# Scores of the second batch from q and k in float32: no squares, no scale and no half-precision words of q and k for batch 1, and a new order of all instructions

## The chip, the core and the metric

The kernel runs on one core of one Trainium2 chip. The core has five instruction streams that run beside each other: TensorE (PE in the profile; its weight loads are PEld), VectorE (DVE), ScalarE (ACT), GpSimd (POOL) and SyncE (SP, which here only issues DMAs). Each takes its instructions strictly in the order in which the program holds them, and waits for the others through semaphores. The metric is the device time of one execution in microseconds (us); the figure given for a kernel is the median of several executions.

## The reference

Causal attention with a decay over 8 batches of 8 heads (576 positions, 64 wide), and behind it a two-layer block over all 4608 tokens:

```python
scores = scale * np.matmul(q, k.transpose(0, 1, 3, 2))
cum = np.cumsum(np.log(np.clip(f, 0.0001, 1.0)), axis=-1)
decay = cum[:, :, :, None] - cum[:, :, None, :]
scores = np.where(causal, -1000000000.0, scores + decay)
scores = scores - np.max(scores, axis=-1, keepdims=True)
attn = np.exp(scores)
attn = attn / (np.sum(attn, axis=-1, keepdims=True) + 1e-09)
x = np.matmul(attn, v)            # then (4608, 512), heads beside each other

h = x @ w_in                      # 512 -> 1024
e = np.exp(h - h.max(-1)); sm = e / (e.sum(-1) + 1e-09)
solu = h * sm
ln = (solu - mean(solu)) / sqrt(var(solu) + 1e-06) * g_ln
out = ln @ w_out                  # 1024 -> 512
```

All inputs and the output are float32.

## The kernel before, in words

**Tiling.** Two heads make a pair; there are 4 pairs in a batch and 32 in all (pair p belongs to batch p // 4 and uses the buffers numbered p % 4). The 576 rows of a pair's scores are cut into five tiles of 64, 128, 128, 128 and 128 rows; tile i has 64 + 128 i columns, and the last one's 576 columns are cut into two of 288. That is 64 + 192 + 320 + 448 + 288 + 288 = 1600 columns per head. The two heads of a pair stand on the two halves of the PE's rows, so that their products run side by side. The block behind the attention works on 36 "layers" of 128 tokens: 24 products into the pair of banks `hps` (lines 919 to 921), a chain on DVE, ACT and POOL, a transpose, and 24 products out (lines 989 to 991).

**Number formats.** Products are made of half-precision words: a float32 number is scaled by a power of two and split into a high and a low float16 word, and a product is three passes (high by high, low by high, high by low). For q and k of a batch this takes: the load into one of four buffers `raws` (`load`, line 761), squares that are summed per partition to find the largest size (`squares`, line 673, on ACT at line 681), one scale for the batch (`scale`, line 628, a chain of small DVE instructions at lines 645 to 670 with two small PE products between), and per pair two high words (POOL, through `copied`, line 503) and two low words (DVE, line 774), made by `split_qk` and written to one of four buffers `qk16`. v is treated in the same way (lines 783 and 784).

**Batch 0 is an exception already.** Its q and k are loaded straight into the `qk16` buffers, used there as float32 (`native`, line 757), and its score products are a single float32 pass (line 819). Since the k words of the other batches carry a factor 16 (`QK`), the score step's own factor (line 841) and the rows of `pick` for the decay term (line 435) differ between batch 0 and the rest. The decay term is one more pass with bfloat16 words (line 817, `pick` and `crow`).

**After the scores.** The reduction with mask and smallest value is on DVE (line 840), the exponential on ACT (line 845), sums on POOL (line 851), the reciprocal on DVE (line 852), the high word of the probabilities on ACT or POOL (lines 501, 503), the low word on DVE (line 867). A DMA from the SP queue transposes them (line 510, `t_p`), the PE multiplies with v (line 889), and ACT and DVE make the two words of x (lines 898, 899).

**Order.** Every step is put into a list as an `Op` with an engine, an estimated cost in ns and the steps it depends on. `Plan.schedule` then lays the list out in time with those costs: of the steps that are ready on an engine it takes the one with the lowest number in the table `RANK` (one number for each step, in the order in which the steps are created). Where the plan leaves the PE without work in its first 300 us, it fills the gap with dummy products of the identity (line 1113, 256 columns each), one for each 256 x 0.4525 ns of planned gap (`FILLED`, `COLUMN`). The program that runs is the plan's order; the chip does not follow the plan's times.

**Buffers.** There are four `raws` and four `qk16` buffers. With `raws`, the load of a later batch may run while the scores of the earlier one still read `qk16`. With the float32 form the load itself goes to `qk16`, and it has to wait until the last score product of the pair that used the buffer is done. All loads and transposes are issued by SP in one order.

Of the kernel before, what the change touches and what calls it, by code (L numbers as in the profile page):

```python
# [15 lines left out]
ALU = mybir.AluOpType  # L16
# [27 lines left out]
NRAW, NQK, NS = 4, 4, 6  # L44
# [5 lines left out]
TURN = (1100.0, 22.0, 1700.0, 6.0)  # L50
# [23 lines left out]
class Plan:  # L74
# [308 lines left out]
def tile_kernel(ctx: ExitStack, tc: tile.TileContext, qk, v, f, w_in, w_out, g_ln, out):  # L383
# [48 lines left out]
    def picks():  # L432
        for n in range(2):
            nc.gpsimd.memset(pick[:, n], -8.0 * QK)
        nc.gpsimd.memset(pick[:, 0, :NPAIR], -8.0)
        for h in range(2):
            for n in range(2):
                x = pick[D * h:D * h + D, n]
# [604 lines left out]
    def whole(p, at, due):  # L1043
        if p >= NPAIR:
            split_qk(p, at + due["split"] + AT_P[p][0])
# [112 lines left out]
```

## Time and profile before

| | us |
|---|---|
| median of 3 runs (lowest, highest) | 698.45 (696.26, 700.66) |
| the profiled execution, whole time | 699.97 |
| its span, first to last instruction | 698.2 |
| PE busy (with the dummy products) | 652.0 |
| DVE busy | 573.9 |
| ACT busy | 532.3 |
| POOL busy | 386.7 |

The span is 1.8 us shorter than the whole time of that execution, and that execution is 1.5 us above the median. Busy time is the time in which at least one instruction of the engine was running. A row of a stage table gives a stretch of the span, its length, and for each engine the busy time and in brackets the number of instructions; a row of a group gives line, engine, operation, tiles and shapes, the count behind x, then the busy time of all of them and the mean ns of one, and last the idle time of the engine just ahead of them with what ended it. A row of the timeline gives the start, the length, and a run of like instructions with its count.

### The profile page before, as it was taken

To read this page: it belongs to the slowest core of one execution; us is meant where nothing else is said; L and a number is where in the kernel's file an instruction comes from. 1 tells how busy PE (TensorE), PEld (TensorE's weight loads), DVE (VectorE), ACT (ScalarE), POOL (GpSimd) and SP (SyncE) were. 2 spreads that over 40 slices of the span, in tenths; PEclk is the share of its full clock that TensorE was granted. 3 is DMA by queue.
4 is the path that set the end of the run, shared out by engine and by line. 5 is a ranking of instruction groups with operands and counts; after the bars stand their busy time and mean duration, and the time that the engine had idled before them with its cause. 6 is when DMAs were issued, how large, how long until landed. Compare 5 with 4: busy or idle time off the path is not lost. (4 is left out here: it accounts for less than half of the span.)

```text
span 698.2 us, 18149 instructions
## 1 busy us (share of the span) xinstructions
PE 652.0 (93%) x6678; PEld 359.3 (51%) x6678; DVE 573.9 (82%) x1685; ACT 532.3 (76%) x1328; POOL 386.7 (55%) x599
## 2 busy tenths in 40 slices
PE   6998799897999999899999999998999999999998
PEld 4775456653554454455454545554455545554455
DVE  6876899989999899799989799999998987565232
ACT  6998756968797896879879887996777887574432
POOL 3020557465567766567657658676477663366410
PEclk9999999999999999999999999999999999999999
DMA  8969158886998999879989997999866895854701
GB/s 331 322 183 268 58 102 204 154 176 115 218 176 193 178 180 197 201 162 169 204 153 213 194 195 149 238 183 163 143 125 124 148 162 106 172 78 94 152 30 46
DMA packets 284281, 116.22 MB, mean 166 GB/s; under 512 B 269856, under 2 KB 270304, under 8 KB 283168
## 3 DMA queue, kind: packets, MB, share of 16 engines
q1 hardware_dynamic: 284192, 115.07, 79.3%
q8 instruction: 52, 0.85, 0.5%
q14 instruction: 37, 0.30, 0.2%
HBM read 38.27 MB, written 9.66 MB: 69 GB/s over the span
## 5 line engine op out<-in xcount | busy, mean ns | idle before, releaser
L845 ACT ACTIVATE p<-p,nm 128x448 f32<-128x448 f32 (+2 forms) x192 | 126.5, 661 | 40.7 <-DVE nm L840 40.5
L851 POOL TENSOR_SCALAR sm<-sm 128x2 f32<-128x2 f32 (+1 forms) x128 | 39.7, 310 | 153.7 <-ACT p L845 111.8
L919 PE MATMUL hps<-wi_h,x_h 128*128 128x512 f16 x288 | 110.3, 383 | 5.6 <-DVE e L937 5.6
L989 PE MATMUL ps<-wo_f,zz 128*128 128x512 f16 x280 | 107.2, 383 | 3.4 <-DVE nm L840 2.7
L921 PE MATMUL hps<-wi_h,x_l 128*128 128x512 f16 x288 | 110.0, 382 | 0.0
L920 PE MATMUL hps<-wi_l,x_h 128*128 128x512 f16 x288 | 110.0, 382 | 0.0
L819 PE MATMUL ps<-qk 64*128 64x320 f16 (+5 forms) x1104 | 99.5, 291 | 11.2 <-DVE nm L840 4.7
L990 PE MATMUL ps<-wo_f,zz 128*128 128x512 f16 x280 | 106.7, 381 | 0.0
L991 PE MATMUL ps<-wo_f,zz 128*128 128x512 f16 x280 | 106.7, 381 | 0.0
L867 DVE SCALAR_TENSOR_TENSOR wo_p<-p,ri,wo_p 128x448 f16<-128x448 f32 (+1 forms) x128 | 101.9, 826 | 2.4 <-ACT wo_p L501 1.8
L889 PE MATMUL ps<-t_p,v 128*64 128x128 f16 (+1 forms) x2880 | 94.5, 219 | 8.5 <-DMA t_p<-p16s 4.0
L889 PEld LDWEIGHTS <-v 128*64 128x64 f16 x2880 | 82.3, 110 | 34.0 <-issue 29.6
L840 DVE CUSTOM_DVE_ANT_0 p<-ps,mask 128x448 f32<-128x448 f32 (+2 forms) x192 | 93.3, 513 | 4.7 <-PE ps L817 4.2
L961 POOL TENSOR_TENSOR z<-e,z 128x1024 f16<-128x1024 f32 x30 | 67.8, 2261 | 28.6 <-ACT z L501 28.4
L930 DVE TENSOR_REDUCE st<-hps 128x1 f32<-128x1024 f32 x36 | 43.7, 1214 | 29.4 <-PE hps L921 29.4
L503 POOL TENSOR_SCALAR wo_p<-p,ri 128x576 f16<-128x576 f32 x64 | 54.4, 856 | 18.8 <-DVE ri L852 14.1
L933 ACT ACTIVATE e<-hps,st,unscale 128x1024 f32<-128x1024 f32 x32 | 38.4, 1200 | 33.9 <-DVE st L931 20.9
L819 PEld LDWEIGHTS <-qk 64*128 64x128 f16 x1008 | 37.8, 94 | 48.4 <-issue 31.4
L503 POOL TENSOR_SCALAR qk<-raws,scale 128x576 f16<-128x576 f32 x56 | 49.0, 881 | 14.8 <-DVE scale L670 5.9
L867 DVE SCALAR_TENSOR_TENSOR p16s<-ps,ri,p16s 128x192 f16<-128x192 f32 (+1 forms) x128 | 38.8, 337 | 16.7 <-ACT p16s L501 16.3
L937 DVE SCALAR_TENSOR_TENSOR e<-hps,e 128x1024 f32<-128x1024 f32 x36 | 43.8, 1217 | 9.6 <-ACT e L933 9.2
L817 PE MATMUL ps<-crow,pick 64*128 64x448 bf16 (+1 forms) x360 | 51.5, 276 | 0.0
(178 smaller groups left out, 1323.6 us busy)
## 6 DMA issues: line engine op xcount, KB each, us to landing
raws<-in_qk_dram SPq DMA_DIRECT2D x28, 576.0 KB, 5.0
vraw<-in_v_dram SPq DMA_DIRECT2D x8, 1280.0 KB, 6.9
out_dram<-y SPq DMA_DIRECT2D x35, 256.0 KB, 2.8
wo_raw<-in_w_in_dram SPq DMA_DIRECT2D x4, 1024.0 KB, 9.7
qk<-in_qk_dram SPq DMA_DIRECT2D x4, 576.0 KB, 12.0
vraw<-in_w_out_dram SPq DMA_DIRECT2D x2, 1024.0 KB, 5.8
t_raw<-in_w_out_dram SPq DMA_DIRECT2D x2, 1024.0 KB, 6.3
t_p<-p16s SPq DMA_TRANSPOSE x96, 3.5
```

The source lines that it names most:

```text
L503: (nc.vector if eng == DVE else nc.gpsimd).tensor_scalar(now(out_), now(in_), scale, 1.0, ALU.mult, ALU.mult)
L819: nc.tensor.matmul(dst, x[row(h), 0, q0:q0 + P], y[row(h), 1, cols], start=(n == 0), stop=False)
L840: op(DVE, R_NS[i] if n == 0 else 442, at[i][h] + STEPS[0], lambda i=i, h=h, n=n, a=a, e=e, x=x, m0=m0: nc.vector.tensor_tensor_reduce(home ...
L845: op(ACT, E_NS[i], at[i][h] + STEPS[1], lambda i=i, h=h, x=x: nc.scalar.activation(home(i, h), home(i, h), AF.Exp, bias=x, scale=-1.0, acc ...
L867: op(DVE, L_NS[j], at[j][g] + STEPS[4], lambda j=j, g=g, nq=nq, h16=h16, l16=l16, r1=r1: nc.vector.scalar_tensor_tensor(l16(), home(j, g, ...
L889: nc.tensor.matmul(o[row(h), a:a + n], v16[m][:, x, 2 * j + h], t[:, y, i + j if h else i - j], start=(j == 0 and c == 0), stop=(j == i an ...
L919: nc.tensor.matmul(hps[:, sl], x_h, wi_h[:, c, sl], start=(c == 0), stop=False)
L920: nc.tensor.matmul(hps[:, sl], x_h, wi_l[:, c, sl], start=False, stop=False)
L921: nc.tensor.matmul(hps[:, sl], x_l, wi_h[:, c, sl], start=False, stop=(c == NCC - 1))
L989: nc.tensor.matmul(o, zz[:, a, 0, j], wo(0, k), start=(k == 0), stop=False)
L990: nc.tensor.matmul(o, zz[:, a, 0, j], wo(1, k), start=False, stop=False)
L991: nc.tensor.matmul(o, zz[:, a, 1, j], wo(0, k), start=False, stop=(k == NFC - 1))
```

## The change

`NAT` (2) is the number of batches whose scores are made from float32 q and k. Batch 1 (pairs 4 to 7) joins batch 0: its q and k are loaded into `qk16`, nothing of them goes through `raws`, `squares`, the q and k columns of `scale`, or `split_qk`; its score products are one float32 pass in the place of three float16 passes. `pick` and the factor of the score step follow. Three costs of the planner are changed as well (a transpose's, a plain DMA's, and two of ACT's), and the whole table `RANK` is replaced, so that every engine's order is another one from the first instructions to the last.

```diff
-NRAW, NQK, NS = 4, 4, 6
+NRAW, NQK, NS, NAT = 4, 4, 6, 2
-TURN = (1100.0, 22.0, 1700.0, 6.0)
+TURN = (1100.0, 25.0, 1700.0, 6.0)
 RANK = (
-    8, 3, 0, 17, 23, 1, 2, 4, 13, 16, 14, 19, 20, 11, 24, 27, 29, 33, 36, 39, 26, 30, 34, 37, 45, 47, 92, 169, 181, 211, 175, 216, 48, 159, 6, 9, 15,
...
-        nc.gpsimd.memset(pick[:, 0, :NPAIR], -8.0)
+        nc.gpsimd.memset(pick[:, 0, :NAT * NPAIR], -8.0)
...
-        op(SP, kb / 0.25, due, lambda: nc.sync.dma_start(out=now(out_), in_=now(in_)), reads, writes, clear=clear)
+        op(SP, kb / 0.3, due, lambda: nc.sync.dma_start(out=now(out_), in_=now(in_)), reads, writes, clear=clear)
...
     def load(p, at):
         b, hp = divmod(p, NPAIR)
-        if b == 0:
-            dma(at, native(hp), qk[b, hp], 576, writes=[(x, hp, j) for x in ("qk", "qkl") for j in range(2)])
+        if b < NAT:
+            dma(at, native(p % NQK), qk[b, hp], 576, writes=[(x, p % NQK, j) for x in ("qk", "qkl") for j in range(2)])
             return
         dma(at, raw[p % NRAW], qk[b, hp], 576, writes=[("raw", p % NRAW)])
...
-            passes = ((x32, x32),) if p < NPAIR else ((hi, hi), (lo, hi), (hi, lo))
+            passes = ((x32, x32),) if p < NAT * NPAIR else ((hi, hi), (lo, hi), (hi, lo))
...
-        ns = 30 + sum((20 if near else 10 if p < NPAIR else 8) * (4.5 + 0.215 * (cuts(i)[1 + (a > 0)] - a)) for i, a in pieces)
+        ns = 30 + sum((20 if near else 10 if p < NAT * NPAIR else 8) * (4.5 + 0.215 * (cuts(i)[1 + (a > 0)] - a)) for i, a in pieces)
...
     def whole(p, at, due):
-        if p >= NPAIR:
+        if p >= NAT * NPAIR:
             split_qk(p, at + due["split"] + AT_P[p][0])
...
-            for j in (1, 2):
+            for j in (1, 2) if b >= NAT else ():
                 squares(b, n, j, at + QDUE[1] + 2 * n)
             squares(b, n, 0, at + VDUE[1])
-        scale_batch(b, 0, 3, at + VDUE[2])
+        scale_batch(b, 0, 3 if b >= NAT else 1, at + VDUE[2])
```

On DVE, at the end of the work on batch 0 (`nm_3` belongs to its last pair, `p_4` is its last tile; `nm_0` is already the first pair of batch 1, `scale_1` is batch 1's scale), there stands before:

```order
L852 RECIPROCAL ri_3_90<-sm_3_94 128x2
L840 ISA p_4_65,nm_3_86<-ps3_146,mask_66,nm_3_86 128x288
L840 ISA nm_3_86 128x1
L774 SCALAR_TENSOR_TENSOR qk16_3_71<-raws_67,scale_1_116,qk16_3_71 128x576
L867 SCALAR_TENSOR_TENSOR wo_1_p16_1229<-p_3_64,ri_3_90,wo_1_p16_1229 128x448
L774 SCALAR_TENSOR_TENSOR qk16_3_71<-raws_67,scale_1_116,qk16_3_71 128x576
L840 ISA ps4_147,nm_0_83<-ps4_147,mask_66 128x64
L840 ISA nm_0_83 128x1
```

and now:

```order
L839 ISA p_4_65,nm_3_86<-ps1_144,mask_66,nm_3_86 128x288
L839 ISA nm_3_86 128x1
L839 ISA p_4_65,nm_3_86<-ps5_148,mask_66,nm_3_86 128x288
L839 ISA nm_3_86 128x1
L839 ISA ps2_145,nm_0_83<-ps2_145,mask_66 128x64
L839 ISA nm_0_83 128x1
```

The low words of batch 1 are gone, and the first reduction of batch 1 follows directly on the last one of batch 0; the low word of probabilities that stood between them comes later.

On SP, at the transposes of batch 0's last two tiles (`t1_0_p` from `wo_0_p16` and `wo_1_p16`, two buffers that the four pairs take in turn), there stands before:

```order
L510 DMA_TRANSPOSE t1_0_p_1149<-wo_1_p16_1229 128x14x128
L510 DMA_TRANSPOSE t1_0_p_1149<-wo_1_p16_1229 128x18x128
L507 DMA out_0_dram<-y_0_139 128x512
L507 DMA raws_67<-in_qk_dram 128x1152
L510 DMA_TRANSPOSE t1_0_p_1149<-wo_0_p16_1130 128x14x128
L507 DMA raws_67<-in_qk_dram 128x1152
L510 DMA_TRANSPOSE t1_0_p_1149<-wo_0_p16_1130 128x18x128
L507 DMA out_0_dram<-y_1_140 128x512
```

and now:

```order
L509 DMA_TRANSPOSE t1_0_p_1129<-wo_0_p16_1107 128x14x128
L506 DMA qk16_1_69<-in_qk_dram 128x1152
L509 DMA_TRANSPOSE t1_0_p_1129<-wo_0_p16_1107 128x18x128
L509 DMA_TRANSPOSE t1_0_p_1129<-wo_1_p16_1194 128x14x128
L506 DMA qk16_2_70<-in_qk_dram 128x1152
L509 DMA_TRANSPOSE t1_0_p_1129<-wo_1_p16_1194 128x18x128
L509 DMA_TRANSPOSE t1_0_p_1129<-wo_0_p16_1107 128x14x128
L509 DMA_TRANSPOSE t1_0_p_1129<-wo_0_p16_1107 128x18x128
L506 DMA qk16_3_71<-in_qk_dram 128x1152
```

The loads to `raws` at this place were those of batch 2 (batch 1's had been issued among the first 16 rows of the queue); now the loads of batch 1 stand here, between the transposes, and the four of batch 2 have taken the early place.

The dummy products number 418 before, 319 of them ahead of the first layer product and 99 behind it; now there are 363, 346 ahead of it and 17 behind. The first layer's 24 products into `hps` stand ahead of the fourth-tile scores of batch 0's third pair in both.

More of the change, by code (lines that the diff above doesn't have):

```diff
@@ L840, in scores @@
                 op(DVE, R_NS[i] if n == 0 else 442, at[i][h] + STEPS[0], lambda i=i, h=h, n=n, a=a, e=e, x=x, m0=m0: nc.vector.tensor_tensor_reduce(
-                    home(i, h)[:, a:e], bank(p, i, h, n)[:, :e - a], mask[:, m0 + a:m0 + e], -0.125 / (QK if p >= NPAIR else 1.0), x if n else BIG, ALU.add, ALU.min, accum_out=x),
+                    home(i, h)[:, a:e], bank(p, i, h, n)[:, :e - a], mask[:, m0 + a:m0 + e], -0.125 / (QK if p >= NAT * NPAIR else 1.0), x if n else BIG, ALU.add, ALU.min, accum_out=x),
                    [score_keys(p, i, h)[n], ("mask",)], [token(i, h), ("nm", m, i, h)], clear=[] if HOME[i] else [("p", i)])
@@ L844, in scores @@
             x = nm[m][:, i, h:h + 1]
-            op(ACT, E_NS[i], at[i][h] + STEPS[1], lambda i=i, h=h, x=x: nc.scalar.activation(
+            op(ACT, E_NS[i] + (28 if i in (2, 3) else 0), at[i][h] + STEPS[1], lambda i=i, h=h, x=x: nc.scalar.activation(
                 home(i, h), home(i, h), AF.Exp, bias=x, scale=-1.0, accum_out=sm[m][:, i, h:h + 1]),
@@ L858, in scores @@
             prior = [("w32", c) for c in (2 * n2, 2 * n2 + 1)] + [("w32", "s", k) for k in range(4 * n2, 4 * n2 + 4)] if p < 2 and j > 2 else []
-            copied(P_HI[j], {POOL: N_NS[j], ACT: 158 + 0.83 * w, DVE: 67 + 1.05 * w}, at[j][g] + STEPS[3], h16, lambda j=j, g=g, nq=nq: home(j, g, nq),
+            copied(P_HI[j], {POOL: N_NS[j], ACT: (158 if HOME[j] else 187) + 0.83 * w, DVE: 67 + 1.05 * w}, at[j][g] + STEPS[3], h16, lambda j=j, g=g, nq=nq: home(j, g, nq),
                    reads, [("p16", n2, j, g)], scale=r1, clear=prior, port=not HOME[j])
```

290 rows, old and new, of the table RANK are left out of this document.

## The prediction

> **What bounds the kernel now.** I read the page's busy times first, then cut the span by events that the timeline shows, and asked for the busy time in each piece. From the timeline of PE, the first layer product and the first score product of batch 2:
>
> ```profile
> 72.95 0.39 PE L919 MATMUL hps<-wi_h,x_h 128*128 128x512 f16 x1
> 178.39 0.26 PE L819 MATMUL ps<-qk 64*128 64x64 f16 x6
> ```
>
> The table by stage, cut there and at 590 us, behind which DVE's share falls; then the same table for the dummy products alone:
>
> ```profile
> core 0: us, PE busy (x) PEld busy (x) DVE busy (x) ACT busy (x) POOL busy (x), PEclk, DMA share, GB/s
> 0.00:73.00 73.00, 60.19 (x617) 45.68 (x618) 52.60 (x158) 63.17 (x151) 13.15 (x47) 0.95 0.93 275
> 73.00:178.40 105.40, 92.49 (x1036) 54.08 (x1036) 98.81 (x288) 77.44 (x195) 62.15 (x96) 0.97 0.65 135
> 178.40:590.00 411.60, 394.87 (x4223) 204.93 (x4222) 374.59 (x1135) 340.60 (x889) 270.07 (x390) 1.00 0.90 173
> 590.00:698.20 108.20, 104.48 (x810) 54.64 (x807) 47.89 (x105) 51.10 (x94) 41.34 (x67) 1.00 0.48 97
> ```
>
> ```profile
> core 0: us, PE busy (x) PEld busy (x), PEclk, DMA share, GB/s
> 0.00:73.00 73.00, 40.83 (x319) 31.36 (x319) 0.95 0.93 275
> 73.00:178.40 105.40, 12.36 (x99) 9.10 (x99) 0.97 0.65 135
> ```
>
> The first 73 us are start-up: two thirds of PE's busy time there is dummies. In the second stage DVE is busy for 98.81 of 105.40 us (94%), while PE has 12.91 us idle and 12.36 us of dummies, 25.3 us without work: DVE sets the pace. In the third PE is busy for 96% and DVE for 91%: nearly a tie, with PE ahead. In the last PE alone is busy (104.48 of 108.20); it works off the layers that are left. A microsecond saved on DVE in stage two therefore brings PE's work forward, and PE, whose work behind 178 us stays the same, would end that much earlier, unless it meets new waits. Batch 1's scores lie in stage two: that is where the change acts.
>
> **What goes.** The groups that make the words of q and k, over all seven batches that do so:
>
> ```profile
> L774 DVE SCALAR_TENSOR_TENSOR qk<-raws,scale,qk 128x576 f16<-128x576 f32 x56 | 48.4, 875 | 0.4 <-POOL qk L503 0.3
> L503 POOL TENSOR_SCALAR qk<-raws,scale 128x576 f16<-128x576 f32 x56 | 49.0, 881 | 14.8 <-DVE scale L670 5.9 <-PE ps L819 4.8 <-PE ps L817 1.4
> L681 ACT ACTIVATE junk<-raws 128x1152 bf16<-128x1152 f32 x28 | 32.5, 1161 | 6.8 <-DMA raws<-in_qk_dram 6.5
> L681 ACT ACTIVATION_READ_ACCUMULATOR junk<-raws 128x1 f32 x28 | 5.4, 193 | 0.0
> ```
>
> Batch 1 has 8 of the 56 and 4 of the 28. DVE loses 8 x 875 ns = 7.0 us, POOL 8 x 881 = 7.0 us, ACT 4 x (1161 + 193) = 5.4 us. The scale chain on DVE shrinks from three columns to one. The first and last row of its first part, for batch 0 (one column) and for batch 1 (three):
>
> ```profile
> 45.84 0.27 DVE L645 TENSOR_REDUCE scale<-ps 1x1 f32<-1x128 f32 x1
> 46.67 0.14 DVE L655 TENSOR_SCALAR scale<-scale 1x1 int32<-1x1 int32 x1
> 88.65 0.55 DVE L645 TENSOR_REDUCE scale<-ps 1x3 f32<-1x384 f32 x1
> 90.58 0.14 DVE L662 TENSOR_SCALAR scale<-scale 1x1 f32<-1x1 f32 x1
> ```
>
> That is 46.81 - 45.84 = 0.97 us against 90.72 - 88.65 = 2.07 us, so 1.1 us less. DVE's term is 7.0 + 1.1 = 8.1 us, all of it from the stage that DVE paces. POOL has room (62.15 of 105.40 us), but POOL's high word is what DVE's low word waits for, so with it a link goes that cost little: 0.4 us of idle time ahead of the DVE group. I credit nothing for POOL. ACT's squares of batch 1 stand in the start-up, where ACT is full:
>
> ```profile
> 20.00:60.00 40.00, 36.20 (x397) 28.07 (x396) 33.47 (x106) 39.62 (x99) 5.73 (x14) 1.00 0.92 241
> ```
>
> ACT is busy for 39.62 of 40 us, so up to 5.4 us could come out of the start-up. The changed order puts the squares of batch 2 ahead of the first layer's exponential, in the place of batch 1's, so I credit nothing, and keep 5.4 us for the low end.
>
> **What comes.** The score products as float32, first as batch 0 has them, then as three float16 passes; the start of the decay pass (L817) marks the end of each:
>
> ```profile
> 51.71 1.02 PE L819 MATMUL ps<-qk 64*128 64x448 f32 x4
> 52.57 0.35 PE L817 MATMUL ps<-crow,pick 64*128 64x448 bf16 x2
> 55.91 0.65 PE L819 MATMUL ps<-qk 64*128 64x288 f32 x4
> 56.39 0.29 PE L817 MATMUL ps<-crow,pick 64*128 64x288 bf16 x2
> 304.61 0.74 PE L819 MATMUL ps<-qk 64*128 64x448 f16 x6
> 305.19 0.35 PE L817 MATMUL ps<-crow,pick 64*128 64x448 bf16 x2
> 309.32 0.53 PE L819 MATMUL ps<-qk 64*128 64x288 f16 x6
> 309.69 0.28 PE L817 MATMUL ps<-crow,pick 64*128 64x288 bf16 x2
> ```
>
> A piece of 448 columns that stands first in its run takes 0.86 us instead of 0.58, 0.63 ns more per column; one of 288 that follows another takes 0.48 instead of 0.37, 0.38 ns more. With 1600 columns a pair and four pairs this is 4.0 us by the one and 2.4 by the other; pieces of both kinds occur, so I take 3.2 us. Its cover is the 25.3 us that PE has free in stage two; without cover it costs the 3.2.
>
> The Trainium skill has a rule that speaks against the change (FP8 and Floating Point Precision, section TensorE Precision Notes): a true float32 product is four passes through the array. By it the float32 form costs a third more than three passes, 0.19 us on the 448-column piece, an estimate of 2.8 us for the four pairs. The trace has more on that piece (0.28 us) and nearly the same on the other (0.11 against 0.12). By the rule the sum below would be 0.2 us lower.
>
> **What moves.** The load of a pair's q and k now waits for the last product of the same pair in batch 0, and stands in SP's one row of DMAs. What is queued behind it there is the next pair's transposes of probabilities, for which PE's value products wait. The times from issue to landing of such loads, in the stream and at the crowded start:
>
> ```profile
> raws<-in_qk_dram SPq DMA_DIRECT2D x28, 576.0 KB, 5.0
> qk<-in_qk_dram SPq DMA_DIRECT2D x4, 576.0 KB, 12.0
> ```
>
> Between a load and its first use there stands, for the last three pairs, at least the work on a whole earlier pair, more than 5.0 us; I take nothing, with 5.0 to 12.0 us a load if the cover is gone. The loads of batch 2 move to the early place that batch 1's had: the same bytes, so nothing either way.
>
> The new order itself is a cost that no row of before shows. It can be bounded by its dummies, since the plan puts one wherever it sees PE without work up to 300 us. Ahead of the first layer product there are 27 more, at 40.83/319 = 128 ns each 3.5 us; behind it 82 fewer, at 12.36/99 = 125 ns each 10.2 us. In the plan PE thus stands idle 6.8 us less on balance, and takes 3.2 us more for float32: PE's account gives -3.6 us, DVE's -8.1.
>
> **The sum.** The two accounts look at the same gain from two engines, and stage two ends by whichever is later, DVE in the trace. But DVE's gain has to pass through stage three, where PE leads. I take the middle, -5.9 us. Against the profiled execution (699.97 us, of which the span is 698.2 and 1.8 lie around it) this is 694.1; that execution is 1.5 us above the median of 698.45, and from the median it is 692.6 us.
>
> **The rivals.** First, *DVE paces on through stage three*, and with it the whole -8.1 us arrives, perhaps the 5.4 us of ACT as well: 690.3 down to 684.9, taken at 687.6. For it speaks that DVE is within 4% of PE in stage three, and PE has 16.73 us idle there which a lighter DVE could fill; against it, PE's full last stage and the dummies ahead of the first layer product. The Trainium skill has the rule that would make this the likely case (Perfetto Trace Analysis, Identifying the Most-Contended Engine): PE is not to be judged by its matmul busy time but by MFU and by weight loading, the others by occupancy. Weight loads fill half of this span, so by that rule DVE would be the engine to relieve throughout. The last stage, DVE 47.89 us against PE 104.48 of 108.20, does not bear it out, and I leave this case at 0.22.
>
> Second, *the gain is spent by the order*: the first layer product comes 3.5 us later, as the dummies say, and PE, which never gets idle again behind it, pays the 3.2 us as well: -8.1 + 3.5 + 3.2 = -1.4, 697.1 us. For it speaks PE's 96% in stage three; against it, the 82 dummies fewer behind the first layer product. Chance 0.20.
>
> Third, on the other side, *the loads hold up SP*: a load whose pair of batch 0 is not done with its scores holds the queue, the transposes behind it start late, PE's value products and then the next reductions on DVE wait. The first load has no transposes of batch 0's last tiles ahead of it; the other three stand among them. Three holds of a landing each are 3 x 5.0 = 15.0 us, the float32 products then lie on the path (3.2), the words are still gone (-8.1): +10.1, 708.6 us. The point from which it decides is a load issued less than 5.0 us ahead of its pair's first product; three such would do. For it speaks that SP is strictly in order; against it, that the value products of whole pairs stand between. Chance 0.13.
>
> That the change does not do what it says can be left out: the changed program has 8 low words and 4 squares fewer and no float16 products in batch 1.
>
> **How the numbers follow.** The forecast has 0.45; its own range runs from -8.1 to -3.6, 690.3 to 694.9. One per cent of the median is 7.0 us, about what a measurement of this kernel can tell from no change (its three runs lie 4.4 us apart), so faster is below 691.5 and slower above 705.4. Faster: nearly all of the first rival (0.20) and a good third of the forecast (0.17), 0.37. Slower: the third rival, 0.13. The rest, 0.50, is within 1%. The range from 685 to 704 takes in the first rival's low end, the forecast and the second rival, with room for one exposed load on top of the latter (697.1 + 5.0 = 702.1), and leaves out the third rival and little else.
>
> **What would show it.** Right would be: 48 low words (L774's successor) and 24 squares in the groups; float32 pieces of 448 columns at 0.86 us, and twice as many of them; stage two, from the first layer product to batch 2's first score, shorter by 5 to 10 us, with hardly a dummy in it; the first layer product 0 to 4 us later than 72.95; the last two stages together as long as before, within 3 us. Wrong: a wait of PE's score products for DMA of over 2 us (third rival), stage two no shorter or the start-up longer by more than 4 us (second), the stage behind it shorter by more than 3 us (first).

## The result and the profile after

The changed kernel takes 681.11 us (median; 680.34 to 681.55), before 697.77 in the same comparison: a ratio of 0.9755, 95% interval 0.9721 to 0.9789. That is 16.7 us less, where 5.9 were forecast, and 3.9 us below the low end of the range. The direction is right, the size is wrong.

The timeline of PE in the kernel after has the two events that cut the stages:

```profile
77.12 0.39 PE L918 MATMUL hps<-wi_h,x_h 128*128 128x512 f16 x1
158.07 0.26 PE L818 MATMUL ps<-qk 64*128 64x64 f16 x6
```

The first layer product comes 4.2 us later than before (72.95), batch 2's first score 20.3 us earlier (178.39). The table by stage of the kernel after, cut at these events, and then the table for the dummy products alone (L1112):

```profile
core 0: us, PE busy (x) PEld busy (x) DVE busy (x) ACT busy (x) POOL busy (x), PEclk, DMA share, GB/s
0.00:77.10 77.10, 66.49 (x658) 49.30 (x658) 60.65 (x182) 69.23 (x160) 19.52 (x57) 0.98 0.88 271
77.10:158.10 81.00, 80.62 (x853) 44.78 (x853) 78.61 (x251) 68.33 (x182) 42.74 (x76) 1.00 0.87 169
158.10:575.00 416.90, 402.64 (x4251) 208.85 (x4250) 375.84 (x1124) 339.84 (x880) 276.46 (x397) 1.00 0.89 172
575.00:678.60 103.60, 98.31 (x822) 52.51 (x820) 52.00 (x118) 51.37 (x101) 35.71 (x62) 1.00 0.47 97
```

```profile
0.00:77.10 77.10, 44.31 (x346) 33.58 (x346) 0.98 0.88 271
77.10:158.10 81.00, 2.27 (x16) 1.40 (x16) 1.00 0.87 169
```

The stages behind batch 2's first score are as long as before (520.5 us against 519.8). The whole gain lies in stage two: 81.0 us instead of 105.4, 24.4 less, of which the start-up gives 4.2 back. In stage two PE had 12.91 us idle and 12.36 us of dummies; now it has 0.38 and 2.27. So PE's free time fell from 25.3 to 2.65 us, 22.6 of the 24.4, and its granted clock rose from 0.97 to 1.00. DVE's busy time there fell by 20.2 us, not by 8.1. Part of that is work that moved into the start-up (DVE 52.60 to 60.65 us) and part is work that moved behind batch 2's first score (422.48 to 427.84 us); the low words of `w_out`, for instance, in the groups of stage two before and after:

```profile
L745 DVE SCALAR_TENSOR_TENSOR wo_f<-wo_f,sg,wo_f 128x512 f16<-128x512 f32 x8 | 6.8, 904 | 0.8 <-POOL wo_f L503 0.8
```

```profile
L744 DVE SCALAR_TENSOR_TENSOR wo_f<-wo_f,sg,wo_f 128x512 f16<-128x512 f32 x3 | 2.2, 738 | 0.0
```

The groups of the kernel after that answer to what goes, and the timeline rows of a float32 piece of batch 1 (448 columns, first in its run: 109.78 - 108.92 = 0.86 us, as in batch 0):

```profile
L773 DVE SCALAR_TENSOR_TENSOR qk<-raws,scale,qk 128x576 f16<-128x576 f32 x48 | 39.6, 839 | 0.5 <-POOL qk L502 0.5
L680 ACT ACTIVATE junk<-raws 128x1152 bf16<-128x1152 f32 x24 | 27.9, 1161 | 5.1 <-DMA raws<-in_qk_dram 4.8 <-ACT junk L946 0.2
```

```profile
108.92 1.02 PE L818 MATMUL ps<-qk 64*128 64x448 f32 x4
109.78 0.36 PE L816 MATMUL ps<-crow,pick 64*128 64x448 bf16 x2
```

What PE waited for in stage two stands in the view of waits (engine, line, what it waited for: us in all, times, longest). Before, and then after, where the one wait left is 0.3 us:

```profile
PE hps L919 <- DVE e L937: 4.1, 1, 4.1
PE ps L977 <- DVE zz L981: 2.1, 1, 2.1
PE ps L989 <- DVE nm L840: 2.1, 1, 2.1
PE ps L819 <- DVE nm L840: 1.4, 4, 0.8
```

```profile
PE ps L888 <- DMA t_p<-wo_p: 0.3, 1, 0.3
```

The first row is layer 1's first product. There is one pair of banks `hps`, and PE stands until DVE has read layer 0's result from it. The timeline of PE from layer 0's last product to layer 1's first shows what the old order has in between (start, length, line, tiles, count, wait ahead), and then what the new one has:

```profile
77.92 0.38 PE L921 MATMUL hps<-wi_h,x_l 128*128 128x512 f16 x1
78.23 0.76 PE L819 MATMUL ps<-qk 64*128 64x288 f32 x4
...
79.43 0.29 PE L817 MATMUL ps<-crow,pick 64*128 64x288 bf16 x2
83.85 0.38 PE L919 MATMUL hps<-wi_h,x_h 128*128 128x512 f16 x1 [4.13 <-DVE e L937]
```

```profile
82.09 0.38 PE L920 MATMUL hps<-wi_h,x_l 128*128 128x512 f16 x1
...
82.73 1.02 PE L818 MATMUL ps<-qk 64*128 64x448 f32 x4
...
83.87 0.86 PE L888 MATMUL ps<-t_p,v 128*64 128x128 f16 x24
...
86.60 0.76 PE L818 MATMUL ps<-qk 64*128 64x288 f32 x4
...
88.02 0.39 PE L918 MATMUL hps<-wi_h,x_h 128*128 128x512 f16 x1
```

Two score products and then a wait of 4.13 us before; three score products, value products and eight dummies, and no wait, after (the elided rows hold the rest). The score products in both are batch 0's, which were float32 already, so the form did not touch them. The wait is there again, 4.1 us long, in *form_old_order_2* below, which has the form and the old order: it went by the order. For the rest of the 22.6 us the two traces can't say whether form or order did it.

### The profile page after: what moved, and what is told of

Same layout as the page of the kernel before. It is cut to its first block, busy times and chain, and to the rows that moved or that the text cites. A ratio compares the mean times of both kernels' runs of the same rounds, so it can differ in the third digit from the quotient of the medians.

```text
span 678.6 us, 17916 instructions
## 1 busy us (share of the span) xinstructions
PE 648.1 (95%) x6573; PEld 355.4 (52%) x6573; DVE 567.1 (84%) x1672; ACT 528.8 (78%) x1320; POOL 374.4 (55%) x591
## 5 line engine op out<-in xcount | busy, mean ns | idle before, releaser
L818 PE MATMUL ps<-qk 64*128 64x288 f16 (+9 forms) x1056 | 105.1, 305 | 11.2 <-DVE nm L839 4.2
L866 DVE SCALAR_TENSOR_TENSOR wo_p<-p,ri,wo_p 128x576 f16<-128x576 f32 (+1 forms) x128 | 104.8, 845 | 3.6 <-POOL wo_p L502 2.1
L960 POOL TENSOR_TENSOR z<-e,z 128x1024 f16<-128x1024 f32 x30 | 66.7, 2222 | 19.1 <-ACT z L500 18.5
L818 PEld LDWEIGHTS <-qk 64*128 64x128 f16 x864 | 32.9, 94 | 39.8 <-issue 26.9
L866 DVE SCALAR_TENSOR_TENSOR p16s<-ps,ri,p16s 64x64 f16<-64x64 f32 (+1 forms) x128 | 38.9, 338 | 14.2 <-ACT p16s L500 13.9
L500 ACT ACTIVATE wo_p<-p,ri 128x448 f16<-128x448 f32 x64 | 40.0, 660 | 13.7 <-DVE ri L851 8.8
```

The source lines that it names most:

```text
L818: nc.tensor.matmul(dst, x[row(h), 0, q0:q0 + P], y[row(h), 1, cols], start=(n == 0), stop=False)
L866: op(DVE, L_NS[j], at[j][g] + STEPS[4], lambda j=j, g=g, nq=nq, h16=h16, l16=l16, r1=r1: nc.vector.scalar_tensor_tensor(l16(), home(j, g, ...
L960: op(Z_LO[n], {DVE: 1280, POOL: 2130}[Z_LO[n]], at, lambda: engine(Z_LO[n]).tensor_tensor(z16[:, :, 1], e2, z16[:, :, 0], ALU.subtract), [ ...
```

## The experiments

Theory A: the new order does most of it, by letting PE and DVE work where they waited for each other. Theory B: the float32 form does it in any order, since it takes the chain of squares, scale and words away from batch 1 (with the forecast's 8.1 us of DVE as its smaller version). To hold the order still, the kernels below (except *float32_twice* and *after_pe_less*, which keep the order of after unchanged) do not plan it anew. They take it from a list of all steps, copied from the plan of before or of after:

```diff
+        todo = list(ORDER)
+        while todo:
+            o = next(self.ops[x] for x in todo if not self.ops[x].left and ...)   # the first in the list that can go
```

In all of these but *form_old_order*, *words_new_order* and *dve_put_back*, PSUM banks and the places of the dummy products are copied as well.

### The form in the old order

*form_old_order* and *form_old_order_2*: the kernel after with the list of before. 20 steps are gone, batch 1's four loads stand behind the scores that free their buffers, and nothing else moves.

```diff
-RANK = (...)                      # of after
+ORDER = (...)                     # the steps as before's plan has them, without the 20
```

> The form alone: batch 1's scores in float32, without squares, scale and words of q and k, but every engine keeps the order of before, instruction for instruction (the 20 steps that go are left out; only the four loads of batch 1 stand later, each behind the last score product of the pair of batch 0 that used its buffer). Theory A (the new order brings most of the gain, by filling the time in which PE and DVE wait for each other ahead of batch 2): only the words and the chain are saved on DVE, 8.1 us at most, so 689 to 696 us, and stage two (first layer product to batch 2's first score) stays above 95 us, with PE's idle time and dummies still there. Theory B (the form itself removes the chain squares, scale, words, scores that held stage two up, and any order would do): 681 to 685 us, stage two near 81 us. Theory C (the loads of batch 1, now behind batch 0's scores, hold SP's queue up in an order not made for them): 700 to 710 us, with waits of PE for DMA ahead of batch 1's scores.

> The form alone, once more: the order of before on every engine as in the run form_old_order, and this time also its dummy products (418) at the places of before and its PSUM banks. Theory A (the new order carries most of the gain): 689 to 697 us, stage two above 95 us. Theory B (the form alone, in any order): 681 to 685 us. If it comes out at 698 or above, the 8.1 us that DVE loses are worth nothing in the old order: something other than DVE's and PE's amount of work holds that order up.

The first, whose dummies were put by the plan's clock into banks in use (so some sums are overwritten), took 700.21 us, ratio 1.0024 (0.9999 to 1.0049). The second took 701.13 us, ratio 1.0036 (1.0009 to 1.0064). Its table by stage, cut at its own first layer product and first score of batch 2:

```profile
0.00:70.30 70.30, 59.98 (x617) 45.70 (x618) 52.64 (x158) 58.91 (x143) 14.13 (x47) 0.95 0.83 256
70.30:175.50 105.20, 96.30 (x986) 55.66 (x987) 91.14 (x275) 77.74 (x196) 54.15 (x88) 0.97 0.71 156
175.50:701.80 526.30, 502.30 (x5031) 260.89 (x5029) 424.65 (x1239) 392.30 (x982) 310.44 (x457) 0.99 0.79 155
```

This is the most telling row of the study. DVE lost 7.7 us of work in stage two (98.81 to 91.14), close to the 8.1 us of the forecast's term, and the stage is as long as before: 105.20 us. Both theories expected too much of the form; theory B is out. DVE was busy for 94% of that stage before, and its amount of work did not set the length. The longest wait of PE in the stage is the one of before:

```profile
PE hps L937 <- DVE e L955: 4.1, 1, 4.1
```

The two times lie at the low end of theory C's range as well, but its sign, waits of PE for DMA, is small: 0.2 us in stage two of the first run and 2.3 us in that of the second, against 1.2 us before, all of them for transposes.

### The order without the form

*words_new_order* and *words_new_order_2*: `NAT = 1` in the order of after. The words of batch 1 are put in ahead of its scores; batch 2's loads, squares and chain have to wait for the four `raws` again. The second has the dummies and banks of after.

```diff
-NRAW, NQK, NS, NAT = 4, 4, 6, 2
+NRAW, NQK, NS, NAT = 4, 4, 6, 1
+ORDER = (...)                     # as after's plan has them, with the 20 put in
```

> The order alone: the instructions of before (batch 1's q and k through squares, scale and words), in the order of after. The 20 steps that after lacks are put in as far ahead of batch 1's scores as they stood before; the four loads of batch 1 go back to the early place, and batch 2's loads, squares of q and k and scale chain, which need the same four buffers, to behind the words of batch 1, as before. Theory A: stage two keeps the gain of the order and pays the 8.1 us of DVE again: 687 to 692 us. Theory B: the words hold stage two up as before: 695 to 703 us. Theory A' (the order is worth something only because the form makes room for it: batch 2's chain moves into the early place): 693 to 700 us, with the loss where batch 2's chain now stands, between batch 1's scores.

> The order alone, once more: words_new_order with the dummy products of after (363) and its PSUM banks. Batch 1's q and k go through squares, scale and words, put in ahead of its scores as before; batch 2's loads, squares and chain stand behind them, for want of buffers. If the loss of the first run (712.0) was the dummies': 687 to 697 us. If the order needs what the form frees: 700 to 712 us, with PE waiting for DVE ahead of batch 1's or batch 2's scores.

712.03 us, ratio 1.0194 (1.0141 to 1.0247), and 704.64 us, ratio 1.0099 (1.0072 to 1.0127). The order alone gains nothing either. Stage two of the second:

```profile
83.50:183.00 99.50, 82.11 (x899) 45.41 (x897) 87.29 (x259) 71.52 (x186) 51.10 (x84) 0.95 0.70 143
```

It is 5.9 us shorter than before and 18.5 longer than after, with 8.7 us more work on DVE than after; the first layer product comes 10.5 us later than before, and behind batch 2's first score the 519.3 us are those of before. The order cannot be had word for word without the form: batch 2's preparation stands early in it, and that needs the buffers that the form leaves free. The words and the later preparation came back together here, so these runs don't part the two, and they don't show what another order made for the words would give.

### Which part of the order

*new_early_old_late*: form, the order of after for all it has ahead of batch 2's first score, the order of before behind. *old_early_new_late*: the other way round.

```diff
+ORDER = early[:first score product of batch 2] + what is left, as late has it
```

> The form, with the order of after (and its dummies) for all that after has ahead of batch 2's first score product, and the order of before for all the rest. If the gain lies in the first two stages alone: 681 to 684 us, the rest behind batch 2's first score within 2 us of 520.5. If the new order of the later stages is needed to keep the gain: 686 to 695 us, with the loss behind that point.

> The form, with the order of before (and its dummies) for all that before has ahead of batch 2's first score product, and the order of after for all the rest. If the gain lies in the first two stages alone: the same as form_old_order_2 within 3 us, stage two above 95 us. If the later order matters: 4 to 12 us below form_old_order_2, and the difference lies behind batch 2's first score.

686.26 us, ratio 0.9805 (0.9770 to 0.9839), and 705.01 us, ratio 1.0081 (1.0049 to 1.0112). The table of the first, stage two and the rest:

```profile
77.80:161.90 84.10, 81.83 (x887) 45.82 (x885) 79.28 (x254) 69.75 (x183) 45.71 (x78) 1.00 0.87 168
161.90:686.40 524.50, 500.83 (x5033) 260.72 (x5029) 422.02 (x1237) 389.82 (x978) 309.34 (x457) 0.99 0.80 155
```

With the form given, the early order alone brings 0.9805 against 1.0036, about 16 of the 19.6 us (0.0281 x 698) that lie between the old order and after. The later order brings nothing with the old early one (1.0081 against 1.0036), and some 3.5 us with the new one (0.9755 against 0.9805). These 3.5 us are not shown to be the later order's: the 524.5 us behind batch 2's first score lie within what kernels of one and the same order show there (last section).

*new_start_old_rest* cuts earlier: the order and the 346 dummies of after up to its first layer product, the order of before from there on.

```diff
+ORDER = after[:first layer product] + what is left, as before has it
```

> The form, with the order of after (and its 346 dummies) up to its first layer product, and the order of before (and its 99 dummies) for all the rest. It holds the work that after moves into the start-up: the words of w_out, batch 2's squares, and 8.2 us of DVE's and 10.7 us of ACT's estimated work in all. Theory I (stage two is shorter because this work is out of it): 684 to 692 us, near new_early_old_late (686.3). Theory G (the interleaving of layer products, scores and words behind the first layer product does it): 697 to 705 us, stage two above 95 us, with the start-up 4 us longer as in after.

702.67 us, ratio 1.0035 (1.0014 to 1.0057). Its row of stage two, and its longest waits of DVE and of PE there:

```profile
78.10:179.60 101.50, 94.89 (x970) 54.62 (x968) 81.29 (x252) 67.59 (x179) 45.83 (x81) 0.95 0.63 133
```

```profile
DVE st L948 <- PE hps L939: 10.6, 2, 6.9
```

```profile
PE hps L937 <- DVE e L955: 4.2, 1, 4.2
```

DVE's bill in stage two is now 81.29 us, 17.5 less than before and close to that of after (78.61). The stage is 101.50 us long, not 81. DVE waits 10.6 us for PE's layer products, and PE 4.2 us for DVE behind layer 0. Moving work out of stage two into the start-up gave 3.9 us, which the longer start-up took back. Theory I is out; theory G, the interleaving behind the first layer product, is what is left. It is where this hybrid and *new_early_old_late* differ: form and start-up are alike, and stage two is 101.50 us in the old order and 84.10 in the new one.

*batch2_early*: the form in the old order, with batch 2's loads, four squares and chain moved into the places of batch 1's (13 steps).

```diff
 ORDER:
+    batch 2's 4 loads and 4 squares where before has batch 1's; its 5 steps of the chain each behind batch 1's for v
-    the same 13 steps where before has them
```

> The form in the order of before (form_old_order_2, 701.1 us), with only batch 2's preparation moved into the places that batch 1's has left: its four loads to the early places of the queue of loads, its four squares of q and k to the places in the start-up, its scale chain right behind the one that batch 1 keeps for v. Theory F (the form pays because it frees the four buffers, so that batch 2 is prepared in the start-up): 686 to 694 us. Theory G (it takes the interleaving of layers, scores and words all through stage two): 697 to 702 us.

701.59 us, ratio 1.0042 (1.0013 to 1.0071): no gain. Freeing the buffers is not enough in itself.

### The dummies

*form_old_no_dummies* and *before_no_dummies* leave out the 99 dummies behind the first layer product.

```diff
-    DUMMY: 418 products, 319 of them ahead of the first layer product
+    DUMMY: 319 products, all ahead of it
```

> form_old_order_2 (the form in the order of before, 701.1 us, where DVE is 7.7 us less busy in stage two and the stage is as long as before, 105.2 us), without the 99 dummy products that the old order has behind the first layer product. Theory D (the dummies stand in PE's row and use up what the form sets free): 688 to 695 us, stage two at 93 to 99 us. Theory E (in the old order PE and DVE wait for each other in turn, whatever either has to do, and the dummies run while PE would wait anyway): 699 to 703 us, with PE's idle time longer by what the dummies took.

> The kernel before without its 99 dummy products behind the first layer product, all else as it was. Theory D: 686 to 694 us. Theory E: 696 to 700 us. If the dummies keep the granted clock up: slower than before, with a lower clock behind 73 us.

698.27 us, ratio 0.9993 (0.9963 to 1.0022), and 703.53 us, ratio 1.0076 (1.0049 to 1.0103). Stage two of the first:

```profile
71.40:176.90 105.50, 88.51 (x887) 48.35 (x888) 91.45 (x275) 77.72 (x195) 54.35 (x88) 0.92 0.70 152
```

and of the second:

```profile
70.80:177.10 106.30, 85.85 (x938) 47.37 (x939) 98.90 (x290) 78.85 (x199) 60.80 (x97) 0.90 0.65 136
```

With the form, the stage keeps its length to 0.3 us without some 12 us of dummies, and the granted clock in it falls from 0.97 to 0.92; without the form it is 0.9 us longer than before, at 0.90. The dummies ran in time that PE would have waited, and held the clock up. Theory D is out. The second run is slower than theory E said, as was expected if the dummies keep the granted clock up; but in its trace the loss lies behind batch 2's first score (523.6 against 519.8 us). So do the 2.9 us by which the first is faster than *form_old_order_2* (519.0 against 526.3 us in traces that lie 5.9 us apart). The order there is the same in all four programs; see the last section.

### Who ends stage two in the new order

*dve_put_back* and *dve_put_back_2* add eight DVE operations to the kernel after; *float32_twice* makes batch 1's float32 pass twice (the decay of batch 0's last tiles is doubled by it, too); *after_dve_less* leaves out eight DVE operations, *after_pe_less* the 48 products of the decay pass.

```diff
+            op(DVE, 735, 0.0, lambda j=j: nc.vector.scalar_tensor_tensor(
+                more, native(m)[:, j], 1.0, crow[:, 0], ALU.mult, ALU.subtract), ...)           # dve_put_back, 2 a pair
-            passes = ((x32, x32),) if p < NAT * NPAIR else ...
+            passes = ((x32, x32),) * (2 if p >= NPAIR else 1) if p < NAT * NPAIR else ...       # float32_twice
+            if j == 4 and p // NPAIR == 1:                                                      # after_dve_less
+                continue
-                for n, (x, y) in enumerate((*passes, (None, None))):
+                for n, (x, y) in enumerate((*passes, *(() if p // NPAIR == 1 else ((None, None),)))):   # after_pe_less
```

> The kernel after, with eight operations on DVE put back where the low words of batch 1 would stand (same size, from the float32 q or k of the pair as loaded and the decay rows, into a buffer that nobody reads; no POOL work, no chain). At some 0.84 us each this is 6.7 us more DVE work ahead of and among batch 1's scores. If DVE still sets the pace of stage two (it is busy for 78.6 of 81.0 us): 5 to 8 us slower than after, 686 to 689 us. If PE sets it (80.6 of 81.0 us): 0 to 2 us slower, 681 to 683 us.

> dve_put_back once more, now with the dummy products and PSUM banks of after (the first run had 51 more dummies, 7.4 us of PE time in the stretch from 80 to 120 us, so its 5.2 us could be PE's). Eight more DVE operations, 6.7 to 7.3 us, ahead of and among batch 1's scores. If DVE is a pacer of stage two in the new order beside PE: 685 to 689 us. If PE alone paces and the loss of the first run was the dummies': 681 to 683 us.

> The kernel after, with the float32 pass of batch 1's scores made twice into the same sums (the decay rows of these pairs are doubled and the score step's factor halved, so the scores stay what they are); the order is that of after. A pass costs 0.86 us per piece of 448 columns that stands first and 0.48 us per piece of 288 that follows, so four pairs of 1600 columns are 10.7 to 12.3 us more PE work. If PE sets the pace of stage two: 9 to 13 us slower than after, 690 to 694 us. If DVE sets it and PE follows: 0 to 5 us slower.

> The kernel after without the 8 low words of probabilities of batch 1's widest tile (128x576, 0.914 us each, 7.3 us of DVE work left out in stage two; the transposes read what the buffer held). If DVE still ends stage two: 674 to 677 us. If PE is full and does (80.6 of 81.0 us busy): 680 to 682 us.

> The kernel after without the decay pass of batch 1's scores (48 products of bfloat16 rows, 7.2 us of PE work left out in stage two; these scores lack the decay). If PE ends stage two: 674 to 677 us. If DVE does: 680 to 682 us. If both runs come out 5 us or more lower, neither engine alone sets the pace, and each waits for the other in turn.

| run | us | ratio to before (95%) | less after's 0.9755, us |
|---|---|---|---|
| dve_put_back | 686.35 | 0.9817 (0.9774 to 0.9861) | +4.3 |
| dve_put_back_2 | 686.94 | 0.9831 (0.9804 to 0.9858) | +5.3 |
| float32_twice | 690.10 | 0.9872 (0.9832 to 0.9913) | +8.2 |
| after_dve_less | 680.44 | 0.9752 (0.9729 to 0.9774) | -0.2 |
| after_pe_less | 681.70 | 0.9776 (0.9748 to 0.9804) | +1.5 |

The last column is the difference of the ratios times 698. The rows of stage two, of *dve_put_back_2*, *float32_twice*, *after_dve_less* and *after_pe_less* in turn:

```profile
78.30:166.10 87.80, 83.89 (x851) 46.46 (x849) 83.45 (x257) 67.05 (x180) 43.12 (x76) 0.97 0.70 152
```

```profile
77.70:169.10 91.40, 91.08 (x949) 52.56 (x948) 81.62 (x254) 69.33 (x183) 42.79 (x78) 1.00 0.77 153
```

```profile
77.50:158.10 80.60, 80.08 (x854) 44.25 (x853) 74.95 (x245) 67.94 (x180) 40.17 (x76) 1.00 0.86 168
```

```profile
77.50:158.10 80.60, 78.26 (x803) 43.16 (x801) 78.82 (x251) 68.11 (x182) 42.07 (x76) 1.00 0.84 169
```

Added work lengthens stage two on either engine: by 6.8 us for eight operations that take 6.4 us on DVE, by 10.4 us for some 10.5 us on PE. Of the 6.8 us only a half is waiting: PE's idle time rose by 3.5 us (0.38 to 3.91), and its busy time by 3.3, at a granted clock of 0.97 instead of 1.00. Work taken away shortens the stage by 0.4 us at most, but less came out of it than the 7 us that were meant: DVE's busy time in it fell by 3.7 us (five of the eight low words lie in the stage), PE's by 2.4. With less on DVE, PE is busy for 80.08 of 80.60 us; with less on PE, DVE is busy for 78.82. This fits two engines that are level; it is argued from their busy shares and not shown. In the old order, too, taking work from DVE changed nothing, and adding work was not tried there; what tells the two orders apart is PE's free time, 25.3 us against 2.65.

*third_batch* makes batch 2 float32 as well, in the order of after, its loads behind batch 1's scores.

```diff
-NRAW, NQK, NS, NAT = 4, 4, 6, 2
+NRAW, NQK, NS, NAT = 4, 4, 6, 3
```

> The kernel after, with batch 2 in float32 as well (squares of q and k, their scale and the words of four more pairs go; its loads stand behind batch 1's scores), the order of after otherwise. This takes 8 low words of 0.84 us from DVE and adds 2.4 to 4.0 us to PE, now in the stage behind. If DVE sets the pace there too: 673 to 677 us. If PE does (402.6 of 416.9 us busy): 681 to 686 us.

681.43 us, ratio 0.9753 (0.9718 to 0.9789): the same as after. DVE's busy time over the whole span fell by 6.5 us (567.09 to 560.57) and PE's rose by 4.0 (648.05 to 652.02); the time did neither. It came out at the low edge of what was expected if PE leads.

### The falls of the clock

*before_gap_dummies* and *before_gap_dummies_2*: before with 72 and with 42 more dummies at its long waits.

```diff
 DUMMY:
+    14 ahead of the value product of pair 2, 14 ahead of layer 2's second transpose, 14 ahead of its first product out
+    30 ahead of layer 1's first product            # before_gap_dummies only
```

> The kernel before with 72 more dummy products, placed where PE waits for over 2 us in the trace of before: 14 ahead of the value product at 63.9 us (gap 2.06 us), 30 ahead of layer 1's first product at 83.85 us (4.13), 14 each ahead of layer 2's second transpose at 163.99 (2.13) and its first product out at 167.31 (2.08). At 0.125 us each they fit the waits. Behind each of these waits (behind the last two together) the granted clock is 0.50 for about 3.4 us. Theory H (the falls of the clock lie on the path): each is worth 1.7 us, so 3 to 5 us faster than before, 693 to 695 us, no clock of 0.83 left in the 10 us stretches from 60 to 170 us. If what PE does behind them is hidden by DVE: the clock stays up and the time stays at 697 to 700 us.

> The kernel before with 42 more dummy products, 14 at each of three waits of PE for over 2 us (value product at 63.9 us, second transpose of layer 2 at 163.99, its first product out at 167.31); the 30 that went wrong in before_gap_dummies are left out. Theory H (a fall of the clock lies on the path): two falls fewer at 1.7 us each, 2 to 4 us faster than before, 694 to 696 us. If they are hidden: 697 to 700 us, with the clock up in the stretches 60 to 70 and 160 to 170 us.

705.22 us, ratio 1.0105 (1.0073 to 1.0137), and 706.58 us, ratio 1.0079 (1.0056 to 1.0103). In the first, 30 dummies found no free bank and went to `hps`, where they waited with the layer product and were added behind the wait. In the second, the clock stayed at full in both stretches where it was to be held up, and batch 2's first score came 1.9 us earlier than before (176.51 against 178.39), about the low end of what theory H expects. But the rest then took 528.8 us instead of 519.8, with the same order of real work. The whole time missed both expectations, and the runs don't settle what a fall costs in it.

## Why the prediction was wrong in size

**The step that failed** is the one on which the sum stood: "DVE sets the pace", read from 98.81 of 105.40 us (94%), and with it "a microsecond saved on DVE in stage two therefore brings PE's work forward". The form took 7.7 us from DVE there and the stage kept its 105.2 us (*form_old_order_2*); with 17.5 us less it kept 101.5 (*new_start_old_rest*), where the new order with the same form and start-up took 84.1 (*new_early_old_late*). What held the old stage two was the order in which PE and DVE waited for each other: PE's row had 12.91 us of waits and 12.36 us of dummies in it, the longest wait being layer 1's for layer 0's reading. An engine that is busy for 94% could still be stretched out by waits when its work was cut. So the DVE half of the sum had its sign by luck: its saving was worth nothing by itself. The other half, the order's, had the right engine and was far too small.

**The second step that failed** is the size of the order. I bounded it by the dummies ("PE thus stands idle 6.8 us less on balance"), since they show where the plan sees PE idle. The plan does not see the chip's waits. What the order could take was all of PE's free time in the trace, and that stood in the prediction: 25.3 us. The new order took 22.6 of it. In hindsight, with 25.3 less the 3.5 us of the later first layer product, the far end of the range would have been -21.8, near 677, and the result inside.

**Point by point.** *What goes* is right in count (48 low words, 24 squares) and in DVE's time (7.7 us measured against 8.1), but worth nothing by itself. *Float32* is right in price on the long piece (0.86 us); the cover of 25.3 us that PE was said to have free for it is wrong for the new order, where 2.65 us of it are left and a second pass cost 8.2 us. *The loads behind SP* at 0 is right: PE waits for none of them in stage two. The five float32 loads issued up to 56 us and the three from 77 us on landed, on the median, close to the two rows that the forecast had (12.0 and 5.0 us):

```profile
qk<-in_qk_dram SPq DMA_DIRECT2D x5, 576.0 KB, 10.7
qk<-in_qk_dram SPq DMA_DIRECT2D x3, 576.0 KB, 4.6
```

*The start-up* at +3.5 us from the dummies is nearly right (+4.2, where 0 to 4 was given as the sign), and *the last two stages as long as before* is right (0.7 us). *Stage two shorter by 5 to 10 us* is wrong (24.4).

**The rivals.** The first (DVE paces on through stage three) had the nearest number, 687.6, but not the cause: its sign, the stage behind shorter by more than 3 us, did not come, and *third_batch* took 8 low words from that stage for nothing. The rule that the prediction set beside it, from the Trainium skill (Perfetto Trace Analysis, Identifying the Most-Contended Engine), looks for the engine to relieve by its occupancy; for DVE in stage two of before these runs show that the occupancy was high and relief was worth nothing. The second rival (the gain is spent by the order) had the order's sign wrong; one of its two signs did come, the start-up longer by more than 4 us (4.2), but stage two gained 24.4 against it. The third (loads hold up SP) did not occur.

## What to carry to other kernels

A high busy share in a stage says that an engine has little room, not that the stage gets shorter when its work does: look for who waits for whom in program order, and count the free time of the other engine, dummies and waits together, as what a new order could take (here it took 22.6 of 25.3 us). A change of form and a change of order can be worth nothing apart and 2.4% together; here the order could not be had without the buffers that the form leaves free. In a stage where PE has 2.65 us of 81 free and DVE is busy for 97%, cutting one engine gained nothing, and adding to either cost most of what was added.

## What was not expected of the hardware

**The clock falls after short waits.** The table of before in stretches of 1 us (PE's busy time, its granted clock, DMA share, GB/s), around a wait of 2.06 us:

```profile
62.00:63.00 1.00, 0.00 (x0) 1.00 0.05 4
63.00:64.00 1.00, 0.10 (x6) 1.00 0.93 162
64.00:65.00 1.00, 1.00 (x11) 0.63 1.32 303
65.00:66.00 1.00, 1.00 (x12) 0.50 0.92 248
66.00:67.00 1.00, 1.00 (x13) 0.50 1.06 394
67.00:68.00 1.00, 1.00 (x9) 0.67 0.95 356
```

In this fall the clock is halved when PE is already at work again, for about 3.4 us (0.37 + 0.50 + 0.50 + 0.33 us lost in these four rows, 1.7 in all). The Trainium skill (TensorE: Matmul & The Clock Gate, section HAM oscillation — how this bites in real kernels) says that it takes idle gaps of more than about 3.4 us; here 2.06 us were enough, so the measurement decides. The kernel before had three such falls from 60 us up to batch 2's first score; the kernel after had none from 20 us up to its last 10 us.

The length of the wait alone does not decide. Before and *form_old_order_2* have the same wait of 2.69 us for DVE; the first two rows are of before, whose clock stays at 1.00, the other two of *form_old_order_2*, whose clock falls:

```profile
474.90 0.26 PE L819 MATMUL ps<-qk 64*128 64x64 f16 x6 [2.69 <-DVE nm L840]
470.00:480.00 10.00, 7.31 (x91) 1.00 0.81 156
476.36 0.26 PE L837 MATMUL ps<-qk 64*128 64x64 f16 x6 [2.69 <-DVE nm L858]
470.00:480.00 10.00, 7.31 (x58) 0.89 0.87 140
```

**Busy time of PE is not its work.** *after_pe_less* leaves out the 48 decay products of batch 1. The table of after for that line alone, over the stretch that holds them:

```profile
102.00:158.00 56.00, 7.18 (x48) 2.82 (x48) 1.00 0.89 179
```

They are busy for 7.18 us, and without them PE's busy time in stage two is only 2.4 us less (80.62 to 78.26). The busy times of neighbouring products overlap. In the timeline of after, the score product shown above (108.92, 1.02 us long) ends at 109.94, the decay pass runs from 109.78 for 0.36 us, and the next product starts ahead of its end:

```profile
110.07 0.39 PE L988 MATMUL ps<-wo_f,zz 128*128 128x512 f16 x1
```

Of the 0.36 us, 0.13 are covered by the decay pass alone. So the busy time of one line is not what leaving the line out sets free.

**What stays open.** Behind batch 2's first score, kernels with the same order there differ by up to 10 us: 519.0 (*form_old_no_dummies*), 519.4 (*new_start_old_rest*), 519.8 (before), 524.5 (*new_early_old_late*), 526.3 (*form_old_order_2*) and 528.8 us (*before_gap_dummies_2*). The three short ones show none or one fall of the clock there, the three long ones two or three. At 1.7 us a fall that is a part of the difference and not all of it; why they come in some programs and not in others is open. This spread lies behind stage two, and it is smaller than the 17 us between the two orders of stage two. That the interleaving in stage two, given the form, is the cause is shown by those two kernels and by what form, start-up, dummies and batch 2's preparation each bring alone; which of its many swaps counts was not tried.
